# A convolution-then-feed-forward kernel: GpSimd's adds go one to a step, a step behind their products, and VectorE's transposes of x go behind the sum of low parts

## The chip, the cores and the metric

The kernel runs on one core of one Trainium2 chip. The metric is the device time of one execution in microseconds (us), as the median of several runs.

## The reference

The computation is a causal convolution along the sequence with seven softmaxed taps per head, followed by a feed-forward layer with a clipped quadratic between its two matrix products. Cut to what matters (the padding of the sequence's start is in x_pad):

```python
# x [8, 4096, 192], weight [8, 7], w_in [192, 2048], w_out [2048, 192]; 8 heads of 24 channels
w = softmax(weight)                                   # over the 7 taps of each head
x = einsum('hk,bskhg->bshg', w, x_unf)                # x_unf: 7 shifted views of x_pad
x = x.reshape(32768, 192)
h = x @ w_in
g = where(h >= 1, h, where(h <= -1, 0, (h + 1)**2 / 4))
out = g @ w_out
```

## The kernel before, in words

**Steps.** The 32768 tokens are cut into 64 groups of 512 tokens (NSB), and the 2048 hidden columns into 8 pairs of 128 (NPAIR). One step q does one pair of one group, so there are 512 steps. The main loop (L967) counts 16 steps, two groups, as one block c; i is the step within the block. Everything is written out in program order; each engine does its own instructions in that order, and semaphores connect the engines.

**TensorE.** In step q it does `mm1(q)` (L448, matmuls at L475), which makes h of pair q, and then `mm2(q-3)` (L511, matmuls at L528), which adds the product of an older g with w_out into four PSUM banks. Both have 36 matmuls of 64 rows by 512 columns, 18 each, and these run in pairs on the two halves of the rows. Numbers are split into a high and a low part (float32r) to keep precision, so `mm1` reads from the convolved x: for the natural layout "n" hi, hi, lo; for the swapped layout "s" hi, hi, lo; then the rest "r". The swapped tiles are copies of hi and lo with the partition halves exchanged, made by two DMAs on SyncE's queue (`swapped`, L252, issues at L255 and L256). h has two buffers, so `mm1(q+2)` waits until the last reader of h(q) is done.

**What the other engines do in step q.** ScalarE: `act_both(q)` (ReLU at L562, square at L563), at i = 2 and i = 10 four copies out of PSUM (`evac_banks`, L609), the products of the convolution (`product`, L237), then `act_hi(q-1)` (L573: gh). VectorE: `act_low(q-2)` (L579: gl), its share of the convolution, `act_sum(q-2)` (L585: the sum of low parts, tile m), transposes of finished output (L631) at i = 0, 7, 8, 15, then `act_most(q)` (L890), the last reader of h(q).

**The convolution** of the next tokens is spread over the steps by tables (PLAN_B, PLAN_A, PLAN_R, L830 to L833), which name what unit b, a or r of a block does at which i: "T" is the transpose of loaded x (L163, VectorE), a number is a tap, "split" makes the high and low part. Unit a holds the first group of a block, b the second (128 channels each), r the other 64 channels of both. Unit a's taps run on VectorE (L230, L232). For b and r ScalarE makes the product of a tap (L237; tap 0 at L244) and GpSimd adds it to y. `conv_slot` (L842) does what the tables say for a step; from the third block of tokens on, the add isn't written at once but put on the list `held`, and `add_held` (L126) writes it behind `act_sum`, with a dependency on it, so that GpSimd starts the add (L129) only when the sum is done.

**Splits.** `splits` (L263) for units a and b: ScalarE copies y to hi (L268), SyncE swaps hi, GpSimd computes lo = y - hi (L272), SyncE swaps lo. `split_rest` (L278) for unit r: ScalarE's copy rh (L282), VectorE's rl = y - rh (L283), and the swaps. The b split stands at i = 5, the first reader of its tiles is `mm1` at i = 8. The a split stands at i = 12 and the r split at i = 13; their first reader is `mm1` at i = 0 of the next block. GpSimd also issues the accumulating DMAs of `evac_add` (L619) at i = 3, 4, 11 and 12.

Of the kernel before, what the change touches and what calls it, by code (L numbers as in the profile page):

```python
# [8 lines left out]
F32 = mybir.dt.float32  # L9
# [22 lines left out]
def lightconv_then_ffn(ctx: ExitStack, tc: tile.TileContext, x, weight, w_in, w_out, out):  # L32
# [24 lines left out]
    nc = tc.nc  # L57
# [53 lines left out]
    def load_unit(c, u, engs=None):  # L111
        ta, tb = 2 * c * TB, (2 * c + 1) * TB
        if u == "rb":
            return load_raw([tb, tb, tb + TB // 2, tb + TB // 2], [P, P + SQ, P, P + SQ], engs,
                            TB // 2)
        if u == "r":
            return load_raw([ta, ta, tb, tb], [P, P + SQ, P, P + SQ], engs)
        return load_raw([ta if u == "a" else tb] * 4, [0, SQ, 2 * SQ, 3 * SQ], engs)
# [2 lines left out]

    pending = []

    held = []

    def add_held(behind):  # L126

        for out, a, b in held:
            add = nc.gpsimd.tensor_add(out, a, b)  # L129
            if behind is not None:  # L130
                tc.add_manual_dep(add.ins, behind.ins.name, mybir.DependencyInfo(
                    mybir.DependencyClass.Sync, mybir.DependencyReason.DATA), reason="port")
        held.clear()

    def let_go():

# [10 lines left out]
    class Conv:  # L147
# [92 lines left out]
        def taps(self, *ks):  # L240
            y = self.y
            for k in ks:
                if k == 0:
                    nc.scalar.mul(y, self.xT[:, SH:SH + TB], wk[:, self.wsel, 0:1])  # L244
                elif self.c == 1 and self.u != "b":
                    pending.append((y, y, self.product(k)))
                elif self.c > 1:
                    held.append((y, y, self.product(k)))
                else:
                    nc.gpsimd.tensor_add(y, y, self.product(k))  # L250

# [4 lines left out]
            nc.sync.dma_start(out=w[BOT].bitcast(F32), in_=t[TOP].bitcast(F32))  # L256
            return w

        def split(self, eng=None):
            for _ in self.splits(eng or nc.gpsimd):  # L260
                pass

        def splits(self, eng):  # L263

            o = xop[2 * self.c + (self.u == "b")]
            hi = xo.tile([P, TB], F32R, name="hi0")
            lo = xo.tile([P, TB], F32R, name="lo0")
            nc.scalar.copy(hi, self.y)  # L268
            for key, t in (("hi", hi), ("lo", lo)):
                if key == "lo":  # L270
                    yield
                    eng.tensor_sub(lo, self.y, hi.bitcast(F32))  # L272
                w = self.swapped(t, key + "1", 3)
                o["n", key] = (t[TOP], t[BOT])
                o["s", key] = (w[TOP], w[BOT])
            yield

        def split_rest(self):  # L278

# [157 lines left out]
    NQ = NSB * NPAIR  # L437
# [63 lines left out]
    turns = tc.alloc_semaphore("turns")  # L501
# [79 lines left out]
    def act_sum(q):  # L581
        gt = stage.tile([P, CC], F32R, name="m")[:, 0:TB]
        gts[q] = gt
        gl = gls[q].bitcast(F32)
        return nc.vector.tensor_add(gt, gl[:, 0, :], gl[:, 1, :])  # L585
# [214 lines left out]
    def whole(j, *cols):  # L800
        for _ in chunks[j].bits(*cols):
# [19 lines left out]
    conv_b, conv_rb = Conv(0, "b", raw_b), Conv(0, "rb", raw_rb)  # L821
# [5 lines left out]

    PLAN_B = {12: ("T",), 14: (0, 1), 15: (2, 3), 1: (4,), 2: (5,), 3: (6,), 5: "split"}  # L830
    PLAN_A = {1: ("T",), 2: (0,), 4: (1,), 6: (2,), 7: (3,), 9: (4,), 10: (5,), 11: (6,),
              12: "split"}
    PLAN_R = {2: ("T",), 4: (0,), 6: (1,), 7: (2,), 8: (3, 4), 9: (5,), 11: (6,), 13: "split"}  # L833
    SECOND_B = {0: (0, 1), 1: (2,), 2: (3,), 3: (4,), 4: (5, 6), 5: "split"}


# [2 lines left out]
    FIRST_A = {7: ("T", 0, 1, 2), 8: (3, 4), 9: (5, 6), 11: "split"}  # L839
    FIRST_R = {8: ("T",), 9: (0,), 10: (1, 2), 11: (3, 4), 12: (5, 6), 13: "split"}  # L840

    def conv_slot(i, b, a, r):  # L842
        early = b is not None and b.c == 0
        plans = ((None if early else b, SECOND_B if b and b.c == 1 else PLAN_B),
                 (a, FIRST_A if early else PLAN_A),
                 (r, FIRST_R if early else PLAN_R))
        for u, plan in plans:
            what = plan.get(i, ()) if u else ()
            if what == "split":
                if u is r:  # L850
                    u.split_rest()
                else:
                    u.split()
                continue
            if "T" in what:
                u.transpose()
            ks = [k for k in what if k != "T"]
            if ks:
                (u.taps_dve if u is a and not early else u.taps)(*ks)
# [8 lines left out]
    def parts_hi(q):  # L868
        for n, rest in PARTS.get(q, ()):
            chunks[n].hi(rest)  # L870
# [95 lines left out]
    conv_n, ahead = {}, {}  # L966
    for q in range(NQ + LATE):  # L967
        s, j = divmod(q, NPAIR)
        c, i = divmod(q, 2 * NPAIR)
        if q < NQ and i == 0 and c > 0:  # L970
            conv_b = conv_n["b"]
        if q < NQ and i == (0 if c > 0 else 4):
            conv_n, ahead = ahead, {}
            if c > 0 and c + 1 < NB:
                for u in "arb":
                    if u not in conv_n:
                        conv_n[u] = Conv(c + 1, u, load_unit(c + 1, u))
        if c == 0 and i in (4, 5, 10):
            u = {4: "a", 5: "r", 10: "b"}[i]
            conv_n[u] = Conv(1, u, load_unit(1, u))  # L980
        if i == (14 if c == 0 else 8) and c + 2 < NB:
            ahead = {u: Conv(c + 2, u, load_unit(c + 2, u)) for u in "ar"}

        done = q - (DELAY if q < NF32 + DELAY else LATE)
        if done < 0 or q == NF32 + DELAY:
            done = None
        if q == NPAIR:
            mm2_first(done)
        if q < NQ:
            mm1(q)  # L990
        if done is not None and q != NPAIR:
            (pair_last if done == NQ - 1 else mm2 if done >= NF32 else mm2_first)(done)

        if q < 2:
            (step_0, step_1)[q]()
        elif q < NPAIR:
            first_step(q)
        elif q < NF32:
            if q == NPAIR + 1:
                evac(0)  # L1000
            if q == 2 * NPAIR - 2:
                pending.extend(late)
            let_go()
            act_clip(q)
            act_square(q)
            parts_hi(q + 1)
            parts_lo(q, (True,))
            let_go()
            act_max(q)
            parts_lo(q, (False,))  # L1010
            conv_slot(i, conv_b, conv_n.get("a"), conv_n.get("r"))
            if j >= NPAIR - 2:
                store(0, "mr"[j - NPAIR + 2])
        else:
            if q == NQ - 1:
                act_hi(q - 1)
            if q < NQ:
                act_both(q)
            if done is not None and done % NPAIR == NPAIR - 1 and done < NQ - 1:
                (evac if done < NF32 else evac_banks)(done // NPAIR)  # L1020
            if done == NQ - 2:
                evac_last(done // NPAIR)
            if q == NF32:
                parts_lo(q)
            n = q - 1 if q < NF32 + 3 else q - 2
            low = n in ghs and n not in gls
            ahead_of = q in (NF32 + 2, NF32 + 3)
            if low:
                act_low(n)
            if ahead_of:  # L1030
                act_most(q)
            if q < NQ:
                conv_slot(i, conv_b if i < 8 else conv_n.get("b"), conv_n.get("a"),
                          conv_n.get("r"))
            add_held(act_sum(n) if low else None)
            if q == NQ - 1:
                act_low(q - 1)
                act_most(q)
                act_sum(q - 1)
            if q < NQ:  # L1040
                if s > 2 and j in (3, 4):
                    evac_add(s - 1, j - 3)
                if s <= 2 or s == NSB - 1:
                    m = 6 if s > 2 else 2
                    if m <= j < m + 2:
                        store(s - 1, "mr"[j - m])
                elif j == NPAIR - 1:
                    store(s - 1, "m")
                if j == 0 and s > 3:
                    store(s - 2, "r")  # L1050
            if q - 1 in gs and q - 1 not in ghs and q < NQ:
                act_hi(q - 1)
            if q < NQ - 1 and not ahead_of:
                act_most(q)
            if q < NF32 + 2:
                act_hi(q)
        if i == 2 * NPAIR - 1 and c == 0:
            conv_n["b"].transpose()
        if q == NQ - 4:
            plain = ob.tile([P, TB // SQ, SQ], F32, name="osb").rearrange("p j b -> p (j b)")[:, 0:P]  # L1060
            diagonal(plain, 0)
# [26 lines left out]
```

## Time and profile before

| what | value |
|---|---|
| median of 3 runs | 2046.57 us (2046.46 to 2049.79) |
| the profiled execution | 2046.76 us, span 2045.0 us |
| PE (TensorE matmul) busy | 2037.9 us, 100% |
| PEld (TensorE weight load) busy | 1756.9 us, 86% |
| DVE (VectorE) busy | 1966.2 us, 96% |
| ACT (ScalarE) busy | 1960.4 us, 96% |
| POOL (GpSimd) busy | 792.8 us, 39% |
| granted TensorE clock | 1.000 |

The span is from the first to the last instruction; the execution's own time lies 1.8 us above it. Busy time is that in which the engine has an instruction in work; records of neighbouring instructions can overlap by some tens of nanoseconds, and matmuls overlap by design.

### The profile page before, as it was taken

The page shows a single profiled execution, that of the slowest core. Times are in us where ns is not written, and L with a number is a line of the kernel's source. Part 1 is how long each engine was busy: PE and PEld are TensorE (multiplying, and loading weights), DVE is VectorE, ACT ScalarE, POOL GpSimd, SP SyncE. Part 2 cuts the span into 40 slices and gives each one's busy share as a digit, 9 for nine tenths or more (in the row PEclk, how much of TensorE's full clock was granted, in tenths as well). Part 3 has the DMA queues.
Part 4 walks back from the last instruction along what each step waited for, and adds up shares of the span by engine and source line. Part 5 has one row for each costly group of instructions (what it writes and reads, how often), then busy time and mean ns, then how long its engine had stood idle before and what let it go on. Part 6 is the DMA issues. An engine that isn't in the chain of part 4 may idle for free.

```text
span 2045.0 us, 46902 instructions
## 1 busy us (share of the span) xinstructions
PE 2037.9 (100%) x18644; PEld 1756.9 (86%) x18644; DVE 1966.2 (96%) x2109; ACT 1960.4 (96%) x2381; POOL 792.8 (39%) x749
## 2 busy tenths in 40 slices
PE   9999999999999999999999999999999999999999
PEld 6998888888888888888888888888888888888888
DVE  8899999999999999999999999999999999999998
ACT  8799999999999999999999999999999999999997
POOL 1544343343433443334434344343343333443431
PEclk9999999999999999999999999999999999999999
DMA  7333333443434434334333344343343433433323
GB/s 178 80 62 70 69 71 71 85 76 56 81 68 79 80 65 77 71 67 87 70 66 73 72 82 76 57 83 69 74 81 65 76 71 66 86 72 65 72 55 55
DMA packets 470685, 152.27 MB, mean 74 GB/s; under 512 B 418944, under 2 KB 426624, under 8 KB 470464
## 3 DMA queue, kind: packets, MB, share of 16 engines
q1 hardware_dynamic: 446880, 109.17, 25.4%
q0 software_dynamic: 23424, 39.99, 13.4%
q8 instruction: 146, 2.39, 0.5%
q14 instruction: 75, 0.61, 0.1%
q10 hardware_dynamic: 160, 0.10, 0.0%
HBM read 32.84 MB, written 25.17 MB: 28 GB/s over the span
## 4 chain that ended last, share of the span: by engine, by line
PE 68%; DVE 15%; ACT 13%; issue 4%; DVEq 0%; ACTq 0%; POOL 0%; POOLq 0%
PE h L475 35%; PE accr L528 20%; PE accm L528 10%; DVE gl L579 7%; DVE g L890 4%; ACT gh L573 3%; ACT g L562 3%; ACT g L563 3%; DVE m L585 3%; ACT p L237 3%; DVE osb L631 1%; PE accm L495 1%; PE accr L495 1%; ACT t L609 0%; ACT y L244 0%
## 5 line engine op out<-in xcount | busy, mean ns | idle before, releaser
L579 DVE TENSOR_TENSOR gl<-g,gh 128x1024 fp32r<-128x1024 f32 x495 | 728.1, 1471 | 23.4 <-ACT gh L573 17.1
L890 DVE SCALAR_TENSOR_TENSOR g<-g,h 128x1024 f32<-128x1024 f32 x504 | 607.5, 1206 | 4.8 <-ACT g L563 2.8
L475 PE MATMUL h<-hi,w 64*128 64x512 f32 x4032 | 609.4, 380 | 1.5
L528 PE MATMUL accr<-gh,wg 64*128 64x512 f32 x3960 | 590.1, 376 | 0.0
L562 ACT ACTIVATE g<-h 128x1024 f32<-128x1024 f32 (+1 forms) x497 | 507.2, 1020 | 41.6 <-PE h L475 39.9
L563 ACT ACTIVATE g<-g 128x1024 f32<-128x1024 f32 (+1 forms) x497 | 526.6, 1060 | 15.8
L573 ACT CAST gh<-g 128x1024 fp32r<-128x1024 f32 x495 | 514.4, 1039 | 0.5 <-DVE g L890 0.4
L129 POOL TENSOR_TENSOR y<-y,p 128x512 f32<-128x512 f32 x180 | 231.0, 1283 | 573.3 <-ACT p L237 300.5
L475 PEld LDWEIGHTS h<-hi,w 64*128 64x128 f32 x4032 | 376.0, 186 | 76.4 <-DVE g L890 28.2
L528 PEld LDWEIGHTS accr<-gh,wg 64*128 64x128 f32 x3960 | 373.9, 185 | 53.2
L129 POOL TENSOR_TENSOR r<-r,p 128x512 f32<-128x512 f32 x180 | 232.5, 1291 | 476.6 <-DVE m L585 420.0
L475 PE MATMUL h<-lo,w 64*128 64x512 f32 x2016 | 383.8, 376 | 0.0
L528 PE MATMUL accr<-gl,words 64*128 64x512 f32 x1980 | 376.3, 376 | 0.0
L585 DVE TENSOR_TENSOR m<-gl 128x512 fp32r<-128x512 f32 x495 | 348.0, 703 | 20.6 <-PE h L475 0.5
L528 PE MATMUL accm<-gh,wg 64*128 64x512 f32 x1980 | 295.1, 376 | 0.0
L475 PE MATMUL h<-rh,w 64*128 64x512 f32 x992 | 293.6, 376 | 0.0
L475 PE MATMUL h<-rhi,w 64*128 64x512 f32 x992 | 293.6, 376 | 0.0
L619 POOL DMA_DIRECT2D t<-t x244 | 206.0, 983 | 97.6 <-DMA t<-t 75.6
L475 PEld LDWEIGHTS h<-lo,w 64*128 64x128 f32 x2016 | 192.2, 186 | 25.9
L528 PEld LDWEIGHTS accr<-gl,words 64*128 64x128 f32 x1980 | 188.3, 186 | 26.0
L528 PEld LDWEIGHTS accm<-gh,wg 64*128 64x128 f32 x1980 | 188.0, 186 | 26.0
L475 PEld LDWEIGHTS h<-rhi,w 64*128 64x128 f32 x992 | 184.5, 186 | 12.9
(161 smaller groups left out, 2313.3 us busy)
## 6 DMA issues: line engine op xcount, KB each, us to landing
t<-t POOLq DMA_DIRECT2D x183, 128.0 KB, 4.1
out_dram<-osb SPq DMA_DIRECT2D x366, 64.0 KB, 1.9
raw<-in_x_dram SPq DMA_DIRECT2D x334, 68.0 KB, 2.6
hi<-hi SPq DMA_DIRECT2D x128, 128.0 KB, 3.4
lo<-lo SPq DMA_DIRECT2D x126, 128.0 KB, 3.1
t<-t POOLq DMA_DIRECT2D x61, 256.0 KB, 3.3
rhi<-rh SPq DMA_DIRECT2D x62, 128.0 KB, 4.1
rlo<-rl SPq DMA_DIRECT2D x62, 128.0 KB, 3.5
```

Of the source, the lines that this page charges most:

```text
L129: add = nc.gpsimd.tensor_add(out, a, b)
L237: nc.scalar.mul(p, self.xT[:, SH + k:SH + k + TB], wk[:, self.wsel, k:k + 1])
L475: nc.tensor.matmul(h[e], w[HALVES[e], c0:c0 + P], seen(x[e][e]), start=(n == 0), stop=(n == len(mms) - 1))
L495: nc.tensor.matmul(accs[s][a, i][:, c0:c0 + D], block, w[half, e, :], start=(j == 0 and e == 0 and b % 2 == 0), stop=(j == NPAIR - 1 and e ...
L528: mm = nc.tensor.matmul(accs[s][bank], w[half], in_turn(g[half]), start=(j == 0 and bank not in seen), stop=(j == NPAIR - 1 and k % 3 == 2 ...
L562: nc.scalar.activation(g[:, e, :], hs[q][:, e, :], AF.Relu, bias=0.5, scale=0.5)
L563: nc.scalar.activation(g[:, e, :], g[:, e, :], AF.Square)
L573: nc.scalar.copy(gh[:, e, :], gs[q][:, e, :])
L579: nc.vector.tensor_sub(gl[:, e, :], g[:, e, :], gh[:, e, :])
L585: return nc.vector.tensor_add(gt, gl[:, 0, :], gl[:, 1, :])
L619: nc.gpsimd.dma_start(out=to, in_=src, accum_op=ALU.add)
L890: nc.vector.scalar_tensor_tensor(out=g, in0=g, scalar=1.0, in1=h, op0=ALU.min, op1=ALU.max)
```

## The change

Three things change, all from the third block of tokens on.

1. Every GpSimd add or subtraction of the convolution is put on the list `fresh`, and moves to `held` when a step ends. So it is written one step after its product, behind that step's `act_sum`, and waits for this sum. This now holds for the lo subtraction of the a and b splits too (with the swap of lo behind it): b's goes from i = 5 to i = 6, a's from i = 12 to i = 13.
2. The tables give at most one product to a step, but for i = 14, where tap 0 is a plain product into y: b's tap 3 goes from i = 15 to i = 0; r's tap 4 from i = 8 to i = 9, and its tap 5 from i = 9 to i = 10.
3. `conv_slot` is called twice in a step: before `add_held` for all but the entries with "T", and behind it for those. So the transpose of loaded x stands behind the sum of low parts.

```diff
--- before.py
+++ after.py
@@ -121,16 +121,17 @@
 
     pending = []
 
-    held = []
+    held, fresh = [], []
 
     def add_held(behind):
 
-        for out, a, b in held:
-            add = nc.gpsimd.tensor_add(out, a, b)
+        for work in held:
+            done = work()
             if behind is not None:
-                tc.add_manual_dep(add.ins, behind.ins.name, mybir.DependencyInfo(
+                tc.add_manual_dep(done.ins, behind.ins.name, mybir.DependencyInfo(
                     mybir.DependencyClass.Sync, mybir.DependencyReason.DATA), reason="port")
-        held.clear()
+        held[:] = fresh
+        fresh.clear()
 
     def let_go():
 
@@ -245,7 +246,7 @@
                 elif self.c == 1 and self.u != "b":
                     pending.append((y, y, self.product(k)))
                 elif self.c > 1:
-                    held.append((y, y, self.product(k)))
+                    fresh.append(lambda p=self.product(k): nc.gpsimd.tensor_add(y, y, p))
                 else:
                     nc.gpsimd.tensor_add(y, y, self.product(k))
 
@@ -256,9 +257,15 @@
             nc.sync.dma_start(out=w[BOT].bitcast(F32), in_=t[TOP].bitcast(F32))
             return w
 
-        def split(self, eng=None):
-            for _ in self.splits(eng or nc.gpsimd):
-                pass
+        def split(self):
+
+            if self.c < 2:
+                for _ in self.splits(nc.gpsimd):
+                    pass
+                return
+            parts = self.splits(nc.gpsimd)
+            next(parts)
+            fresh.append(lambda: next(parts))
 
         def splits(self, eng):
 
@@ -266,14 +273,15 @@
             hi = xo.tile([P, TB], F32R, name="hi0")
             lo = xo.tile([P, TB], F32R, name="lo0")
             nc.scalar.copy(hi, self.y)
+            sub = None
             for key, t in (("hi", hi), ("lo", lo)):
                 if key == "lo":
                     yield
-                    eng.tensor_sub(lo, self.y, hi.bitcast(F32))
+                    sub = eng.tensor_sub(lo, self.y, hi.bitcast(F32))
                 w = self.swapped(t, key + "1", 3)
                 o["n", key] = (t[TOP], t[BOT])
                 o["s", key] = (w[TOP], w[BOT])
-            yield
+            yield sub
 
         def split_rest(self):
 
@@ -827,10 +835,11 @@
 
 
 
-    PLAN_B = {12: ("T",), 14: (0, 1), 15: (2, 3), 1: (4,), 2: (5,), 3: (6,), 5: "split"}
+    PLAN_B = {12: ("T",), 14: (0, 1), 15: (2,), 0: (3,), 1: (4,), 2: (5,), 3: (6,), 5: "split"}
     PLAN_A = {1: ("T",), 2: (0,), 4: (1,), 6: (2,), 7: (3,), 9: (4,), 10: (5,), 11: (6,),
               12: "split"}
-    PLAN_R = {2: ("T",), 4: (0,), 6: (1,), 7: (2,), 8: (3, 4), 9: (5,), 11: (6,), 13: "split"}
+    PLAN_R = {2: ("T",), 4: (0,), 6: (1,), 7: (2,), 8: (3,), 9: (4,), 10: (5,), 11: (6,),
+              13: "split"}
     SECOND_B = {0: (0, 1), 1: (2,), 2: (3,), 3: (4,), 4: (5, 6), 5: "split"}
 
 
@@ -839,13 +848,15 @@
     FIRST_A = {7: ("T", 0, 1, 2), 8: (3, 4), 9: (5, 6), 11: "split"}
     FIRST_R = {8: ("T",), 9: (0,), 10: (1, 2), 11: (3, 4), 12: (5, 6), 13: "split"}
 
-    def conv_slot(i, b, a, r):
+    def conv_slot(i, b, a, r, turns=None):
         early = b is not None and b.c == 0
         plans = ((None if early else b, SECOND_B if b and b.c == 1 else PLAN_B),
                  (a, FIRST_A if early else PLAN_A),
                  (r, FIRST_R if early else PLAN_R))
         for u, plan in plans:
             what = plan.get(i, ()) if u else ()
+            if turns is not None and turns != ("T" in what):
+                continue
             if what == "split":
                 if u is r:
                     u.split_rest()
@@ -1030,9 +1041,11 @@
             if ahead_of:
                 act_most(q)
             if q < NQ:
-                conv_slot(i, conv_b if i < 8 else conv_n.get("b"), conv_n.get("a"),
-                          conv_n.get("r"))
+                units = conv_b if i < 8 else conv_n.get("b"), conv_n.get("a"), conv_n.get("r")
+                conv_slot(i, *units, turns=False)
             add_held(act_sum(n) if low else None)
+            if q < NQ:
+                conv_slot(i, *units, turns=True)
             if q == NQ - 1:
                 act_low(q - 1)
                 act_most(q)
```

How this moves instructions is seen at three places, one on each of three engines. In the rows lines of the changed kernel have other numbers: L249 is the add of before's L129, L280 the lo subtraction of L272, L627 the accumulating DMA of L619, L617 the copy out of PSUM of L609, L238 the product of L237, L581 gh of L573, L570 and L571 ReLU and square of L562 and L563, L275 and L290 the copies hi and rh of L268 and L282, L256 and L257 the swaps of L255 and L256.

GpSimd's queue before, from b's split at i = 5 to a's split at i = 12 of one block (r and y are the tiles that taps are added to, p a product, t the finished sums; DVE, Activation, Pool in the brackets are the engines waited for):

```order
L272 TENSOR_TENSOR lo_8939<-y,hi_8938 128x512 [waits DMAHW4_49,DMAHW5_49,PE_49,Activation_49]
L129 TENSOR_TENSOR r<-r,p 128x512 [waits DVE_49,Activation_49]
L129 TENSOR_TENSOR r<-r,p 128x512 [waits DVE_49,Activation_49,Pool_49] x2
L129 TENSOR_TENSOR r<-r,p 128x512 [waits Activation_49,Pool_49]
L129 TENSOR_TENSOR r<-r,p 128x512 [waits DVE_49,Activation_49,Pool_49] x2
L619 DMA t<-t 128x512 [waits DMASW7_49,DMASW6_49]
L619 DMA t<-t 64x512 [waits DMASW1_49]
L272 TENSOR_TENSOR lo_9352<-y,hi_9351 128x512 [waits DMAHW6_49,DMAHW7_49,PE_49,Activation_49]
```

The same stretch of GpSimd's queue in the changed kernel:

```order
L280 TENSOR_TENSOR lo_8939<-y,hi_8938 128x512 [waits DMAHW0_49,DMAHW1_49,DVE_49,Activation_49]
L249 TENSOR_TENSOR r<-r,p 128x512 [waits DVE_49,Activation_49]
L249 TENSOR_TENSOR r<-r,p 128x512 [waits DVE_49,Activation_49,Pool_49] x4
L627 DMA t<-t 128x512 [waits DMASW7_49,DMASW6_49]
L627 DMA t<-t 64x512 [waits DMASW1_49]
L249 TENSOR_TENSOR r<-r,p 128x512 [waits DVE_49,Activation_49,Pool_49]
L627 DMA t<-t 64x512 [waits DMASW0_49]
L627 DMA t<-t 64x512
L280 TENSOR_TENSOR lo_9348<-y,hi_9347 128x512 [waits DMAHW6_49,DMAHW7_49,DVE_49,Activation_49]
```

The lo subtraction waits for VectorE where it did not, and the add that had no wait for VectorE (the second of a step) has one. The last add of r goes behind the first two accumulating DMAs, and a's lo subtraction behind all four.

ScalarE's queue before, at i = 10 of one block, where the four copies out of PSUM stand, and up to r's split at i = 13:

```order
L563 ACTIVATE g<-g 128x1024
L609 COPY t<-accr_6934 128x512
L609 COPY t<-accr_6935 128x512
L609 COPY t<-accm_6932 128x512
L609 COPY t<-accm_6933 128x512
L573 CAST gh<-g 128x1024
L562 ACTIVATE g<-h 128x1024
L563 ACTIVATE g<-g 128x1024
L237 ACTIVATE p<-r,wk 128x512
L573 CAST gh<-g 128x1024
```

ScalarE's queue in the changed kernel, the same place:

```order
L571 ACTIVATE g<-g 128x1024
L617 COPY t<-accr_6933 128x512
L617 COPY t<-accr_6934 128x512
L617 COPY t<-accm_6931 128x512
L617 COPY t<-accm_6932 128x512
L238 ACTIVATE p<-r,wk 128x512
L581 CAST gh<-g 128x1024
L570 ACTIVATE g<-h 128x1024
L571 ACTIVATE g<-g 128x1024
L238 ACTIVATE p<-r,wk 128x512
L581 CAST gh<-g 128x1024
```

One product more stands between the copies and gh; it came from i = 9.

SyncE's queue before, the swaps at i = 12 and 13 of one block:

```order
L255 DMA hi_7484<-hi_7481 64x512 [waits DMAHW2_49,PE_49,Activation_49]
L256 DMA hi_7484<-hi_7481 64x512 [waits DMAHW3_49]
L255 DMA lo_7488<-lo_7482 64x512 [waits DMAHW4_49,PE_49,Pool_49]
L256 DMA lo_7488<-lo_7482 64x512 [waits DMAHW5_49]
L255 DMA rhi<-rh 64x512 [waits DMAHW6_49,PE_49,Activation_49]
L256 DMA rhi<-rh 64x512 [waits DMAHW7_49]
L255 DMA rlo<-rl 64x512 [waits DMAHW0_49,DVE_49,PE_49]
L256 DMA rlo<-rl 64x512 [waits DMAHW1_49]
```

And in the changed kernel:

```order
L256 DMA hi_7480<-hi_7477 64x512 [waits DMAHW2_49,PE_49,Activation_49]
L257 DMA hi_7480<-hi_7477 64x512 [waits DMAHW3_49]
L256 DMA rhi<-rh 64x512 [waits DMAHW4_49,PE_49,Activation_49]
L257 DMA rhi<-rh 64x512 [waits DMAHW5_49]
L256 DMA rlo<-rl 64x512 [waits DMAHW6_49,DVE_49,PE_49]
L257 DMA rlo<-rl 64x512 [waits DMAHW7_49]
L256 DMA lo_7551<-lo_7478 64x512 [waits DMAHW0_49,Pool_49]
L257 DMA lo_7551<-lo_7478 64x512 [waits DMAHW1_49]
```

The swap of a's lo goes behind the swaps of rh and rl.

## Rows read from the trace of the kernel before

**Rows 1.** Windows (us; PE, PEld, DVE, ACT, POOL busy, count): steady stretch; i = 3 to 7, block 13.

```profile
150.00:1900.00 1750.00, 1747.42 (x16030) 1507.45 (x16028) 1701.09 (x1754) 1702.31 (x2032) 693.67 (x635) 1.00 0.39 73
849.89:869.31 19.42, 19.42 (x182) 17.02 (x180) 18.79 (x20) 19.26 (x25) 8.52 (x8) 1.00 0.36 62
```

**Rows 2.** Waits, whole run: engine line <- releaser: us in total, times, longest.

```profile
PEld h L475 <- DVE g L890: 28.2, 83, 0.5
DVE rl L283 <- ACT rh L282: 15.0, 21, 1.0
```

**Rows 3.** Groups by line, whole run: busy us, mean ns of one.

```profile
L579 DVE TENSOR_TENSOR gl<-g,gh 128x1024 fp32r<-128x1024 f32 x495 | 728.1, 1471 | 23.4 <-ACT gh L573 17.1
```

**Rows 4.** Timeline, turn from block 12 to 13: start us, us, engine [idle before <-releaser].

```profile
839.32 2.65 POOL L129 TENSOR_TENSOR y<-y,p 128x512 f32<-128x512 f32 x2 [2.16 <-ACT p L237]
840.77 2.28 DVE L579 TENSOR_TENSOR gl<-g,gh 128x1024 fp32r<-128x1024 f32 x1
845.76 1.22 DVE L579 TENSOR_TENSOR gl<-g,gh 128x1024 fp32r<-128x1024 f32 x1
845.89 0.30 PEld L475 LDWEIGHTS h<-hi,w 64*128 64x128 f32 x4 [0.45 <-DVE g L890]
```

**Rows 5.** Timeline, b's split in block 13 to the first mm1 that reads it.

```profile
863.29 1.04 ACT L573 CAST gh<-g 128x1024 fp32r<-128x1024 f32 x1
863.47 1.28 POOL L272 TENSOR_TENSOR lo<-y,hi 128x512 fp32r<-128x512 f32 x1 [0.23 <-ACT hi L268]
864.36 1.47 DVE L579 TENSOR_TENSOR gl<-g,gh 128x1024 fp32r<-128x1024 f32 x1
864.83 1.82 SPq L255 DMA_DIRECT2D lo<-lo  x1
865.75 0.74 DVE L232 SCALAR_TENSOR_TENSOR y<-xT,wk,y 128x512 f32<-128x512 f32 x1
866.41 0.68 DVE L585 TENSOR_TENSOR m<-gl 128x512 fp32r<-128x512 f32 x1
867.24 1.28 POOL L129 TENSOR_TENSOR r<-r,p 128x512 f32<-128x512 f32 x1 [2.49 <-DVE m L585]
869.31 0.59 PE L475 MATMUL h<-hi,w 64*128 64x512 f32 x4
870.39 0.38 PE L475 MATMUL h<-lo,w 64*128 64x512 f32 x2
```

**Rows 6.** Tile lo, 150 to 1900 us: first swap's issue (ns, min/median/max), both swaps' landing.

```profile
L255 SPq DMA_DIRECT2D lo<-lo x56: 461/502/1817, 173.8 to 1899.2; - x56
DMA to landing us min/median/max: 2.2/3.1/4.2
```

**Rows 7.** Timeline of ACT, ReLUs of i = 2 to 6 and i = 10 in block 13.

```profile
848.15 1.02 ACT L562 ACTIVATE g<-h 128x1024 f32<-128x1024 f32 x1 [0.54 <-PE h L475]
853.63 1.05 ACT L562 ACTIVATE g<-h 128x1024 f32<-128x1024 f32 x1
857.22 1.01 ACT L562 ACTIVATE g<-h 128x1024 f32<-128x1024 f32 x1
860.78 1.01 ACT L562 ACTIVATE g<-h 128x1024 f32<-128x1024 f32 x1
864.24 1.01 ACT L562 ACTIVATE g<-h 128x1024 f32<-128x1024 f32 x1
879.23 1.02 ACT L562 ACTIVATE g<-h 128x1024 f32<-128x1024 f32 x1
```

**Rows 8.** Timeline, r's split (i = 13) in block 11, and mm1 of i = 15.

```profile
765.06 1.01 ACT L562 ACTIVATE g<-h 128x1024 f32<-128x1024 f32 x1
767.70 0.69 DVE L283 TENSOR_TENSOR rl<-r,rh 128x512 fp32r<-128x512 f32 x1 [0.73 <-ACT rh L282]
768.91 1.21 DVE L890 SCALAR_TENSOR_TENSOR g<-g,h 128x1024 f32<-128x1024 f32 x1
770.42 0.59 PE L475 MATMUL h<-hi,w 64*128 64x512 f32 x4
```

## The prediction

> **What bounds the kernel now.** Begin with the table: all of TensorE, VectorE and ScalarE are busy for 96% or more at a full clock, so look next at how evenly TensorE's steps follow each other. The windows give that. In the steady stretch 16030 matmuls take 1750 us; at 36 to a step that is 3.930 us a step, 62.88 us a block of 16. The five steps of block 13 in the second row take 19.42 us, 3.885 us each, with TensorE busy throughout: this is a step in which nothing makes it wait [rows 1]. So stalls are worth 16 x 0.045 = 0.72 us a block, some 22 us in all (31 blocks have the full program). This is all that any relief of VectorE, ScalarE or GpSimd can give back; the rest is matmul work that the change leaves alone.
>
> The waits tell where the stalls come from. TensorE's weight loads wait 83 times for `act_most` on VectorE, 28.2 us [rows 2] (more than the stalls, since a weight load normally sits a little ahead of its matmul). Why VectorE is late is seen at the turn of a block: two adds follow each other on GpSimd, 2.65 us, and gl, which takes 1.22 us when GpSimd is quiet, takes 2.28 us beside them; two steps later TensorE waits for `act_most` [rows 4]. Over the run gl takes 1.47 us in the mean [rows 3].
>
> **The change, part by part.** Four things are priced: what VectorE gets back, what the later lo of unit b costs, what the product moved to i = 10 costs, and the later lo of unit a.
>
> *VectorE.* A GpSimd operation costs it what is left of that operation when gl wants to start: in block 13 gl starts at 864.36, the lo subtraction runs to 864.75 (863.47 + 1.28), and gl takes 1.47 us [rows 5] instead of 1.22, 0.25 more; behind two adds it takes 2.28, 1.06 more [rows 4]. An add that the sum releases starts 0.15 us behind its end (866.41 + 0.68 = 867.09, to 867.24) and also takes 1.28 us [rows 5], so it outlasts `act_most` a little, and I price it at the same 0.25. After the change no step has two adds: two steps a block (i = 8 and 15) gain 0.8 each. A transpose between sum and `act_most` (0.73 us by its shape's neighbour, the tap at 865.75 [rows 5], which has as many elements) covers what the add has left: three steps (i = 1, 2, 12) gain 0.25. That is 2.4 us of VectorE a block. It lies off TensorE's path except in the stalls, so its worth is between nothing and 0.72 us; since the stall that the rows show comes from such a pair, I take all of it: **-0.72 us a block**. The transposes themselves are first read a step or two later, under work of those steps; without that cover each would cost its 0.7 us.
>
> *The later lo of unit b.* Before, the lo subtraction starts at 863.47, when the cast hi is done, and its first swap is issued at 864.83. Its first swapped reader is `mm1` of i = 8, which starts at 869.31 and comes to the swapped lo with its sixth pair of matmuls, at 870.39 [rows 5]: the lo had time to spare. After the change it waits for the sum of the next step, at 866.41 in this block. That sum can move forward only a little: gl starts at 864.36, as soon as ScalarE's gh ends (863.29 + 1.04), and this stays. Without GpSimd beside it gl takes 1.22 us, so tap and sum come 0.25 us earlier and the sum ends at 866.84. GpSimd then starts at 866.99, ends at 868.27; SyncE issues 0.08 us later, 868.35, as at 864.83 [rows 5]. An issue takes 0.50 us [rows 6], so the second swap goes out at about 868.90. Landing takes 2.2 to 4.2 us, 3.1 in the middle [rows 6]. At 2.2 us it lands at 871.10 and TensorE stalls 0.7 us; at 3.1 us, 1.6 us. I take 2.4 us, since the swaps of hi and the accumulating DMAs, beside which the old ones ran, are through by then: 871.30, a stall of 0.9 us, and an estimated 0.1 us to be at pace again (the weight loads that end such a wait take 0.30 us for four [rows 4], and part of that lies open): **+1.0 us a block**. No other engine's slack can hide this: TensorE works its queue in order, and the rest of `mm1` and `mm2` stands behind that pair. On GpSimd only r's first add, a step later, stands behind the wait, and on SyncE the stores of i = 7: nobody waits for those. The Trainium skill, DMA: Bandwidth & Descriptors, section "Anatomy of one DMA", gives 2.0 us fixed plus bytes over 436 GB/s, fitted for DMAs that GpSimd issues; for these 128 KB that is an estimate of 2.3 us. By it the stall would be 0.8 + 0.1 us, 3 us less over the run; the trace's least, 2.2, agrees, its median doesn't, and I go by the rows.
>
> *The product at i = 10.* ScalarE comes to i = 2 idle, waiting for h (its ReLU at 848.15), and its next ReLU comes 5.48 us later: the four copies and a product. Steps with a product then take 3.59 (853.63 to 857.22), the step with the cast hi 3.46 (860.78 to 864.24) [rows 7]. At i = 10 it starts as promptly: at i = 2 its ReLU is 1.74 us ahead of the next `mm1` (848.15 to 849.89 [rows 1, 7]), and 869.31 + 3 x 3.885 - 1.74 is 879.23, where the ReLU stands [rows 7]. But before the change it has the copies without a product; with the change it has both, so it should run as at i = 2: ReLUs of 11, 12 and 13 at 5.48, 9.07 and 12.53 us after that of 10. Unit r's split follows the ReLU of 13: rl starts 2.64 us behind it (765.06 to 767.70), having waited for rh, and `act_most` ends 5.06 us behind it (768.91 + 1.21) [rows 8], so at 17.59. TensorE would start `mm1` of i = 15 unhindered at 21.16 - 3.885 = 17.28: from the ReLU of i = 2 to `mm1` of i = 8 it is 869.31 - 848.15 = 21.16 us [rows 5, 7], and 10 to 15 is one step less. A stall of 0.31 us, and with the release and the same refilling some 0.15 more: **+0.46 us a block**. In block 11 before, the same chain ended 0.30 us ahead of `mm1` (770.12 to 770.42) [rows 8].
>
> *The later lo of unit a* goes behind the swaps of rh and rl on SyncE's queue. In the times of the last paragraph, counted from the ReLU of i = 10, rl starts at 15.17 and `act_most` 1.21 later (767.70 to 768.91 [rows 8]), at 16.38, about when the sum ends; 0.15 + 1.28 for the subtraction, 0.08 + 0.50 to the second issue and 3.1 to land give 21.5. `mm1` of the next block's i = 0 would start unhindered at 21.16, six steps behind that ReLU, and comes to swapped lo 1.08 later (869.31 to 870.39 [rows 5]), at 22.24. So I take nothing; at 4.2 us, the longest landing [rows 6], it would be 0.4 us a block.
>
> *The sum.* -0.72 + 1.0 + 0.46 = +0.74 us a block; 30 blocks have the new order: +22 us on a span of 2045.0. With the 1.8 us around it, which also brings the profiled execution to the median shown, **2069 us**.
>
> **The rivals.**
> - *Only the lo swap counts.* If ScalarE recovers more before i = 13, the second stall is gone: -0.72 + 1.0 = +0.28, 8 us more, 2055. For it: TensorE's first stall in the block gives every engine 1.0 us; against it: ScalarE comes to i = 10 idle either way.
> - *Slow landings.* At the median of 3.1 us instead of 2.4 the swap costs 1.7 us: +1.44 a block, 43 us, 2090. For it: the median is measured; against it: those DMAs shared the queues.
> - *The swap is hidden: faster.* If the second swap lands within 1.5 us of its issue (870.39 - 868.90), or TensorE comes to `mm1` of i = 8 0.9 us later for a reason that I don't see, only the second stall stays: -0.26 a block, 2039; without it too, -0.72, 2025. Against it: no landing of lo took under 2.2 us [rows 6].
> - *Nothing changes.* The least landing (0.7 us) and no second stall: +0.0, 2047. For it: each size is within its rows; against it: both must hold.
>
> **How the numbers follow.** Both waits as sized: 0.55. Only the lo swap: 0.16. Slow landings: 0.09. Faster: 0.10 (0.06 at 2039, 0.04 at 2025). Nothing: 0.10. A measurement of this kernel can tell 0.2%, about 4 us, from no change. So faster 0.10, same 0.10, slower 0.80. The range goes from the case of nothing, 2046, to 2086, where landings take about 2.9 us and the second stall stands; the faster cases and the slowest landings are left out.
>
> **What would show it.** The lo subtraction starts right behind the sum of i = 6, some 2.3 us before `mm1` of i = 8. TensorE waits for the DMA lo there in every block, 25 to 35 us in all, the longest in its list of waits. rl waits for rh in every block, about 1 us each time, against 15.0 us in 21 waits before [rows 2]. TensorE waits for `act_most` at i = 15, and no longer at i = 2. gl's mean falls from 1.47 us to about 1.3. The prediction is wrong if TensorE has no wait for lo, because the sum comes earlier than I let it or because swaps alone on the queues land in well under 2.2 us; and its size is wrong with the landing.

## The result and the profile after

| | before | after |
|---|---|---|
| median of 5 runs | 2046.77 us (2046.46 to 2049.79) | 2064.92 us (2064.30 to 2065.30) |
| span of the profiled execution | 2045.0 us | 2063.1 us |
| PE, DVE, ACT, POOL busy | 100%, 96%, 96%, 39% | 100%, 91%, 95%, 38% |

The changed kernel is slower: ratio 1.0086, 95% interval 1.0073 to 1.010, 18 us. 2069 us was forecast.

The window of the steady stretch in the changed kernel (columns as in [rows 1]):

```profile
150.00:1900.00 1750.00, 1745.73 (x15869) 1573.55 (x15867) 1597.96 (x1738) 1686.96 (x2011) 679.92 (x627) 1.00 0.40 72
```

15869 matmuls at 36 to a step make 3.970 us a step, 63.52 us a block, against 62.88 before and 62.16 without stalls. So stalls went from 0.72 to 1.36 us a block, 0.64 more. The starts of `mm1` in the trace say where (from each to the next, less 3.885 us, as a mean over blocks 2 to 30): the changed kernel loses 0.78 us a block at i = 8, 0.47 at i = 14 and 0.10 at i = 15, and next to nothing elsewhere. VectorE's share fell and TensorE's stayed at 100%: a pipelined engine that waits half a microsecond here and there still counts as busy, and the count of matmuls in a stretch tells more than the share.

The waits of the changed kernel name what stands where. Beside them gl's group (columns as in [rows 2] and [rows 3]):

```profile
DVE rl L291 <- ACT rh L290: 25.7, 31, 1.0
PEld h L483 <- DMA lo<-lo: 24.5, 59, 0.5
PEld h L483 <- DVE g L901: 12.5, 31, 0.5
PEld accm L536 <- DVE m L593: 10.2, 30, 0.3
```

```profile
L587 DVE TENSOR_TENSOR gl<-g,gh 128x1024 fp32r<-128x1024 f32 x495 | 634.9, 1283 | 118.5 <-ACT gh L581 113.9
```

TensorE's 83 waits for `act_most` are down to 31, one a block. The wait for the DMA lo is new (59 times, two a block), and the sum m is now late once in every block (before: `PEld accm L528 <- DVE m L585: 8.5, 22, 0.6`). gl is down from 1.47 to 1.28 us, so VectorE got back what it was to get; it now stands idle 113.9 us for ScalarE's gh.

The first stall, as the timeline of block 13 shows it, i = 6 to the end of i = 8:

```profile
871.11 1.04 ACT L581 CAST gh<-g 128x1024 fp32r<-128x1024 f32 x1
872.19 1.23 DVE L587 TENSOR_TENSOR gl<-g,gh 128x1024 fp32r<-128x1024 f32 x1
873.33 0.74 DVE L233 SCALAR_TENSOR_TENSOR y<-xT,wk,y 128x512 f32<-128x512 f32 x1
873.99 0.68 DVE L593 TENSOR_TENSOR m<-gl 128x512 fp32r<-128x512 f32 x1
874.81 1.28 POOL L280 TENSOR_TENSOR lo<-y,hi 128x512 fp32r<-128x512 f32 x1 [3.97 <-ACT p L238]
876.12 0.46 SPq L256 DMA_DIRECT2D lo<-lo  x1
876.62 0.60 SPq L257 DMA_DIRECT2D lo<-lo  x1
877.13 0.60 PE L483 MATMUL h<-hi,w 64*128 64x512 f32 x4
878.36 0.18 PEld L483 LDWEIGHTS h<-lo,w 64*128 64x128 f32 x1 [0.39 <-DMA lo<-lo]
878.98 0.18 PEld L483 LDWEIGHTS h<-lo,w 64*128 64x128 f32 x1 [0.44 <-DMA lo<-lo]
881.78 0.70 PE L483 MATMUL h<-hi,w 64*128 64x512 f32 x4
```

Read it from the top: gh ends, gl starts at once, tap, sum. The subtraction starts 0.14 us behind the sum's end (874.67); the trace puts this down to a product of ScalarE that ended between, but that isn't an operand of the subtraction, which waits for the cast hi, done in the step before, and for the sum. Two swaps go out. The sixth pair of matmuls is due at 877.13 + 1.08 = 878.21, and its weight loads wait for the first swap and then for the second, until 878.98. `mm1` of the next step comes 4.65 us later instead of 3.885. The swaps now go out when those of hi are through, and they land sooner than before, with a median of 2.3 us instead of 3.1 (tile lo, 150 to 1900 us):

```profile
DMA to landing us min/median/max: 2.2/2.3/4.3
```

The second stall, block 13, from the ReLU of i = 10 to `mm1` of the next i = 0:

```profile
887.92 1.02 ACT L570 ACTIVATE g<-h 128x1024 f32<-128x1024 f32 x1 [0.23 <-PE h L483]
893.39 1.05 ACT L570 ACTIVATE g<-h 128x1024 f32<-128x1024 f32 x1
896.98 1.01 ACT L570 ACTIVATE g<-h 128x1024 f32<-128x1024 f32 x1
900.45 1.01 ACT L570 ACTIVATE g<-h 128x1024 f32<-128x1024 f32 x1
901.21 0.70 PE L483 MATMUL h<-hi,w 64*128 64x512 f32 x4
903.09 0.69 DVE L291 TENSOR_TENSOR rl<-r,rh 128x512 fp32r<-128x512 f32 x1 [0.82 <-ACT rh L290]
904.30 1.21 DVE L901 SCALAR_TENSOR_TENSOR g<-g,h 128x1024 f32<-128x1024 f32 x1
904.44 0.19 PEld L536 LDWEIGHTS accm<-m,words 64*128 64x128 f32 x2 [0.34 <-DVE m L593]
905.57 0.30 PEld L483 LDWEIGHTS h<-hi,w 64*128 64x128 f32 x4 [0.40 <-DVE g L901]
909.56 0.59 PE L483 MATMUL h<-hi,w 64*128 64x512 f32 x4
```

ScalarE's ReLUs come 5.47, 3.59 and 3.47 us apart, rl waits for rh, and behind rl both the sum and `act_most` are late for TensorE. `mm1` of i = 14, 15 and 0 start at 901.21, 905.57 and 909.56: 4.36 and 3.99 us instead of 3.885, 0.58 together.

### The profile page after: what moved, and what is told of

Its sections match the earlier page's. It is cut to its first block, busy times and chain, and to the rows that moved or that the text cites. A ratio compares the mean times of both kernels' runs of the same rounds, so it can differ in the third digit from the quotient of the medians.

```text
span 2063.1 us, 46868 instructions
## 1 busy us (share of the span) xinstructions
PE 2054.3 (100%) x18644; PEld 1841.6 (89%) x18644; DVE 1871.6 (91%) x2109; ACT 1962.2 (95%) x2381; POOL 785.3 (38%) x749
## 4 chain that ended last, share of the span: by engine, by line
PE 67%; ACT 14%; DVE 9%; issue 4%; DMA 3%; POOL 2%; SPq 1%; ACTq 0%; DVEq 0%; POOLq 0%
PE h L483 34%; PE accr L536 20%; PE accm L536 10%; DVE gl L587 5%; ACT gh L581 4%; DMA lo<-lo 3%; ACT p L238 3%; ACT g L570 3%; ACT t L617 2%; POOL lo L280 2%; DVE g L901 2%; DVE y L233 1%; DVE m L593 1%; PE accm L503 1%; PE accr L503 1%
## 5 line engine op out<-in xcount | busy, mean ns | idle before, releaser
L587 DVE TENSOR_TENSOR gl<-g,gh 128x1024 fp32r<-128x1024 f32 x495 | 634.9, 1283 | 118.5 <-ACT gh L581 113.9
L536 PE MATMUL accr<-gh,wg 64*128 64x512 f32 x3960 | 635.9, 377 | 0.0
L570 ACT ACTIVATE g<-h 128x1024 f32<-128x1024 f32 (+1 forms) x497 | 507.1, 1020 | 57.2 <-PE h L483 57.1
L571 ACT ACTIVATE g<-g 128x1024 f32<-128x1024 f32 (+1 forms) x497 | 525.8, 1058 | 15.8
L581 ACT CAST gh<-g 128x1024 fp32r<-128x1024 f32 x495 | 512.5, 1035 | 0.5 <-DVE g L901 0.4
L483 PEld LDWEIGHTS h<-hi,w 64*128 64x128 f32 x4032 | 418.6, 186 | 47.5 <-DVE g L901 12.5
L536 PEld LDWEIGHTS accr<-gh,wg 64*128 64x128 f32 x3960 | 406.5, 185 | 38.1
L483 PE MATMUL h<-lo,w 64*128 64x512 f32 x2016 | 435.1, 379 | 4.5 <-DMA lo<-lo 2.2
L249 POOL TENSOR_TENSOR y<-y,p 128x512 f32<-128x512 f32 x180 | 231.3, 1285 | 522.4 <-DVE m L593 269.0
L536 PE MATMUL accr<-gl,words 64*128 64x512 f32 x1980 | 419.0, 376 | 0.0
L249 POOL TENSOR_TENSOR r<-r,p 128x512 f32<-128x512 f32 x180 | 231.7, 1287 | 459.6 <-DVE m L593 269.5
L483 PEld LDWEIGHTS h<-lo,w 64*128 64x128 f32 x2016 | 231.7, 186 | 40.1 <-DMA lo<-lo 24.5
L536 PEld LDWEIGHTS accr<-gl,words 64*128 64x128 f32 x1980 | 230.2, 186 | 16.2
L536 PEld LDWEIGHTS accm<-gh,wg 64*128 64x128 f32 x1980 | 215.2, 186 | 16.3
L627 POOL DMA_DIRECT2D t<-t x244 | 206.6, 983 | 31.3 <-ACT t L617 16.3
L536 PE MATMUL accm<-m,words 64*128 64x512 f32 x990 | 213.9, 382 | 0.0
```

The costliest lines, as they stand in the source:

```text
L249: fresh.append(lambda p=self.product(k): nc.gpsimd.tensor_add(y, y, p))
L483: nc.tensor.matmul(h[e], w[HALVES[e], c0:c0 + P], seen(x[e][e]), start=(n == 0), stop=(n == len(mms) - 1))
L536: mm = nc.tensor.matmul(accs[s][bank], w[half], in_turn(g[half]), start=(j == 0 and bank not in seen), stop=(j == NPAIR - 1 and k % 3 == 2 ...
L570: nc.scalar.activation(g[:, e, :], hs[q][:, e, :], AF.Relu, bias=0.5, scale=0.5)
L571: nc.scalar.activation(g[:, e, :], g[:, e, :], AF.Square)
L581: nc.scalar.copy(gh[:, e, :], gs[q][:, e, :])
```

## The experiments

Theory: the time lost is the sum of two waits that the change makes, one for b's swapped lo (4.65 - 3.885 = 0.77 us a block) and one for r's rl (0.58 us), each with its own cause; the old stalls are gone. The expectations put the two at 0.755 and 0.57 us. The rival in each case is that a wait only takes the place of another engine's lateness, or that its cause is another part of the change. Ratios are to the kernel before, run beside each.

### b's lo at once

```diff
         def split(self):
-            if self.c < 2:
+            if self.c < 2 or self.u == "b":
                 for _ in self.splits(nc.gpsimd):
                     pass
                 return
```

> The changed kernel, with unit b's lo subtraction and its swap back at i = 5, in one go with the cast, as before the change; all else as changed. Theory (two new waits, each at its own price): the wait for the DMA lo at i = 8, 0.755 us a block in the changed kernel's trace, goes, and the 0.57 us at i = 14 and 15 stay: 2064.9 - 30 x 0.755 = 2042 us (2038 to 2046), no wait of TensorE for lo. Rival (the wait for lo only takes the place of VectorE's lateness, which comes back at i = 9 to 13 when it is gone): 2050 to 2062 us, with TensorE's waits for act_most up by 10 us or more.

Measured: 2039.85 us (2039.69 to 2040.03), ratio 0.9966 (0.9954 to 0.9978). The window of the steady stretch and TensorE's waits:

```profile
150.00:1900.00 1750.00, 1749.99 (x16086) 1526.94 (x16086) 1622.56 (x1760) 1710.42 (x2040) 689.41 (x636) 1.00 0.41 73
```

```profile
PEld h L483 <- DVE g L901: 12.5, 31, 0.5
PEld accm L536 <- DVE m L593: 10.6, 30, 0.4
```

The wait for lo is gone, and what stays are the 31 and 30 waits of the second stall. 16086 matmuls are 62.67 us a block, 0.51 above the stall-free 62.16. With this one line undone the rest of the change is a gain: 25 us less than the changed kernel.

### b's lo a step later, but without the dependency on the sum

```diff
-            if behind is not None:
+            if behind is not None and work not in free:
                 tc.add_manual_dep(done.ins, behind.ins.name, ...)
...
             fresh.append(lambda: next(parts))
+            if self.u == "b":
+                free.append(fresh[-1])
```

`free` is a new list, empty at first; what stands in it does not wait for the sum.

> The changed kernel; unit b's lo subtraction still written a step later, but without the dependency on the sum, so that it starts when ScalarE's cast hi is done. Theory (the wait for the sum is what makes the swap late): as with b's lo at once, 2040 us (2038 to 2043), the wait of TensorE for lo gone. Rival (the later place in the queues of GpSimd and SyncE makes it late, not the wait): 2060 to 2066 us.

Measured: 2039.71 us (2039.11 to 2041.02), ratio 0.9965 (0.9952 to 0.9978), no wait of TensorE for lo. So it is not the place in the queues but the wait for the sum that makes the swap late.

### r's table of before

```diff
-    PLAN_R = {2: ("T",), 4: (0,), 6: (1,), 7: (2,), 8: (3,), 9: (4,), 10: (5,), 11: (6,),
-              13: "split"}
+    PLAN_R = {2: ("T",), 4: (0,), 6: (1,), 7: (2,), 8: (3, 4), 9: (5,), 11: (6,), 13: "split"}
```

> The changed kernel with unit r's table of before: taps 3 and 4 both at i = 8, tap 5 at i = 9, none at i = 10; adds a step behind, so two of them at i = 9. Theory: ScalarE's product behind the four copies at i = 10 is the cause of the waits at i = 14 and 15, so they go, 0.57 us a block: 2064.9 - 17 = 2048 us (2045 to 2053; the two adds at i = 9 may give some of it back), and rl waits for rh much less than 25.7 us. Rival (VectorE itself is late there, by the adds and the transpose moved behind the sum): 2062 to 2067 us, rl's wait as long as now.

Measured: 2050.47 us (2049.82 to 2051.13), ratio 1.0016 (1.0007 to 1.0026). TensorE's and VectorE's waits:

```profile
DVE rl L291 <- ACT rh L290: 29.4, 31, 1.0
PEld h L483 <- DMA lo<-lo: 24.8, 58, 0.7
PEld h L483 <- DVE g L900: 0.7, 2, 0.5
```

The second stall is gone with the product at i = 10, and only the one for lo is left, now up to 0.7 us in one wait: by the starts of `mm1`, i = 8 loses 0.90 us a block instead of 0.78, and no other step loses time. In one thing the expectation missed: rl's wait for rh is not shorter but longer, 29.4 us. It is no measure of the stall: VectorE comes to rl earlier and waits longer, while rh itself is done 1.25 us behind the start of `mm1` of i = 14 in the median, not 1.85 as in the changed kernel, early enough for TensorE.

### r's table of the change on the kernel before

The same edit the other way round, on the kernel before, whose adds stand in their own step.

> The kernel before with unit r's table of the change alone (one tap at i = 8, 9, 10, 11 each; adds in their own step, lo at once, transposes in front). Theory (the product behind the four copies at i = 10 is enough to make rh, rl and act_most of i = 13 late): waits of 0.57 us a block at i = 14 and 15 as in the changed kernel, against some 0.4 us that one add at i = 8 and the later cast of hi at i = 12 give back: 2051 us (2046 to 2058). Rival (the product only hurts together with adds that come a step later): 2034 to 2041 us.

Measured: 2048.66 us (2048.16 to 2049.35), ratio 1.0008 (0.9998 to 1.0018). Its waits:

```profile
PEld h L475 <- DVE g L891: 38.4, 106, 0.8
DVE rl L283 <- ACT rh L282: 22.7, 31, 1.0
PEld accm L528 <- DVE m L585: 4.0, 26, 0.2
```

Inside the theory's bounds and outside the rival's: the product makes the lateness without any add behind its step. TensorE waits 106 times for `act_most` instead of 83. By the starts of `mm1` it loses 0.49 us a block at i = 12 to 15, not at i = 14 and 15 alone. Before, it lost 0.23 there, through sums held up at i = 12 (see the transposes alone, below), and none is held up here. What the second add at i = 8 cost before, 0.21 us at i = 9 to 11, is saved but for 0.02, and the product takes it back.

### Both tables of before

Both tables set back in the changed kernel, which leaves the adds a step behind and the transposes behind the sum.

> The changed kernel with both tables of before (unit b's taps 2 and 3 at i = 15, unit r's 3 and 4 at i = 8): adds a step behind their products, two of them at i = 0 and i = 9, lo behind the sum, transposes behind the sum. Theory: the wait for lo stays as with unit r's table alone, and VectorE has a microsecond to spare at i = 0 to 2 for the second add: 2050 us (2048 to 2054). Rival (two adds in a step cost a stall wherever they stand): 2057 to 2062 us.

Measured: 2050.19 us (2050.03 to 2050.81), ratio 1.0018 (1.0009 to 1.0028), as with r's table alone. Two adds in one step, a step later, cost TensorE nothing here; whether they would without its wait for lo was not tried.

### The transposes alone

The third part of the change by itself on the kernel before: `conv_slot` in two halves around `add_held`.

> The kernel before with the third part of the change alone: transposes of loaded x behind the sum of low parts. Theory: VectorE gains about 0.25 us at i = 1 and 2, but TensorE's wait at the turn of a block comes from the two adds at i = 15, earlier; at i = 12 the transpose stands behind a sum that the lo subtraction still holds up: 2044 to 2048 us, no difference that can be told. Rival (the transposes in front of the sum are what makes act_most late): 2035 to 2041 us.

Measured: 2039.44 us (2039.14 to 2041.05), ratio 0.9962 (0.9950 to 0.9974). The theory was wrong and the rival right in size. The theory had named the place that matters, i = 12, but took the sum to be held up there with or without the move. In the kernel before, at i = 12 of block 12, with TensorE's `mm1` of i = 13 and its waits behind the sum:

```profile
825.59 0.59 PE L475 MATMUL h<-hi,w 64*128 64x512 f32 x4
826.32 0.73 DVE L163 STREAM_TRANSPOSE xT<-raw 128x544 f32<-128x544 f32 x1
826.92 1.37 POOL L272 TENSOR_TENSOR lo<-y,hi 128x512 fp32r<-128x512 f32 x1
826.98 1.87 DVE L585 TENSOR_TENSOR m<-gl 128x512 fp32r<-128x512 f32 x1
828.90 0.19 PEld L528 LDWEIGHTS accm<-m,words 64*128 64x128 f32 x2 [0.53 <-DVE m L585]
830.04 0.30 PEld L475 LDWEIGHTS h<-hi,w 64*128 64x128 f32 x4 [0.40 <-DVE g L890]
```

With the transposes alone moved, the same place in the same block, where TensorE has no such wait:

```profile
825.87 0.69 DVE L585 TENSOR_TENSOR m<-gl 128x512 fp32r<-128x512 f32 x1
826.28 1.43 POOL L272 TENSOR_TENSOR lo<-y,hi 128x512 fp32r<-128x512 f32 x1
826.48 0.74 DVE L163 STREAM_TRANSPOSE xT<-raw 128x544 f32<-128x544 f32 x1
```

In front of the sum the transpose took just so long that the sum came 0.06 us behind a's lo subtraction and waited it out, 1.87 us instead of 0.69. Ten sums of the 495 took over 1.8 us in the kernel before, none with the transposes moved: there the sum is 0.40 to 0.69 us ahead of the subtraction in every block, and the transpose, at 0.74 us, is not held up beside it. That makes 62.66 us a block (16088 matmuls in the same 1750 us) instead of 62.88, 7 of the 22 us of old stalls.

The starts of `mm1` show that these ten sums are the cause. In each of the ten blocks TensorE loses some 0.57 us at i = 13 (825.59 to 830.04 above: 4.45 us instead of 3.885) and 0.10 at i = 14, 6.7 us together. In the other nineteen of blocks 2 to 30 it loses nothing there, and with the transposes moved in no block. At i = 1 and 2, where the other transposes moved, it loses 0.32 us a block in both kernels, so the 0.25 us that the prediction gave to each of those brought TensorE nothing.

### b's lo at once, and r's taps at i = 5 to 9

```diff
-            if self.c < 2:
+            if self.c < 2 or self.u == "b":
...
-    PLAN_R = {2: ("T",), 4: (0,), 6: (1,), 7: (2,), 8: (3,), 9: (4,), 10: (5,), 11: (6,),
-              13: "split"}
+    PLAN_R = {2: ("T",), 4: (0,), 5: (1,), 6: (2,), 7: (3,), 8: (4,), 9: (5,), 11: (6,),
+              13: "split"}
```

> The changed kernel with b's lo at i = 5 at once, and unit r's taps 1 to 5 at i = 5 to 9, so that no step has two adds and i = 10 has no product. Theory: both waits go and nothing comes in their place, since no step has two adds: 62.2 us a block, 2064.9 - 30 x 1.32 = 2025 us (2022 to 2031), faster than the kernel before by 1%. Rival (ScalarE and VectorE, at 95% and 91%, are the bound as soon as these waits go): 2035 to 2045 us with TensorE's waits for act_most above 15 us.

Measured: 2025.27 us (2024.59 to 2025.53), ratio 0.9892 (0.9875 to 0.9909): 1.1% faster than the kernel before, 1.9% faster than the changed one. The window of the steady stretch:

```profile
150.00:1900.00 1750.00, 1750.00 (x16218) 1530.14 (x16216) 1634.26 (x1776) 1721.21 (x2054) 693.36 (x639) 1.00 0.41 74
```

16218 matmuls are 3.885 us a step, as in the five steps without a wait [rows 1]. Nothing came in place of the two waits, though ScalarE is busy for 98% of this stretch.

### The same, with the transposes in front of the sum

```diff
-                conv_slot(i, *units, turns=False)
+                conv_slot(i, *units)
             add_held(act_sum(n) if low else None)
-            if q < NQ:
-                conv_slot(i, *units, turns=True)
```

> The version with b's lo at once and unit r's taps at i = 5 to 9 (2025.3 us), its transposes of loaded x in front of the sum again. Theory: without two adds in a step VectorE has room for the 0.25 us that each of three adds then costs it: 2025 to 2027 us. Rival (the transposes' place is worth as much here as it was on the kernel before, 7.6 us): 2031 to 2035 us.

Measured: 2026.09 us (2025.90 to 2026.34), ratio 0.9899 (0.9884 to 0.9913). With a's lo behind the sum no sum is held up at i = 12 any more (none of the 495 took over 0.8 us), and the transposes' place is worth under 1 us.

## Why the prediction was right, point by point

- *What bounds it* was right: all that the change could give back was 0.72 us a block, and the version without both waits gives back just that, 2046.8 to 2025.3 us.
- *VectorE's gain* had the right worth and only part of the right cause. All of the 0.72 us went. But the prediction laid it to steps with two adds. By the starts of `mm1` the kernel before loses 0.32 us a block at i = 1 and 2, behind the two adds of i = 15; 0.21 at i = 9 to 11, behind those of i = 8; and 0.23 at i = 13 and 14, through the sums that a's lo subtraction held up at i = 12, which the prediction did not look at. The last goes with the transposes alone, and the second with r's table alone. The first goes with the whole change, and no run shows by itself that the two adds made it; with both tables of before, two adds standing a step later, it is gone too. So that the total came out right was partly luck: the bound was right, and what lay under it was not all of one kind.
- *b's lo*: the chain held link by link, and the wait for the sum is shown as its cause by taking away that wait alone. The size was too large, 1.0 against 0.77 us. The second swap was issued 1.59 us ahead of its need (876.62 to 878.21), not 1.49; TensorE went on 2.36 us behind that (878.98), where 2.4 was taken; and the 0.1 us for getting back to pace was not seen. The Trainium skill, DMA: Bandwidth & Descriptors, section "Anatomy of one DMA", gave an estimate of 2.3 us for the landing, by a fit for DMAs that GpSimd issues, and the trace after agrees with its median of 2.3; for the swaps of the kernel before, with a median of 3.1, it is too short.
- *The product at i = 10*: ReLUs at 5.48, 9.07 and 12.53 us were foreseen and came at 5.47, 9.06 and 12.53; rl and `act_most` followed at 2.64 and 5.06 us as foreseen. The size was too small, 0.46 against 0.58 us, since TensorE was due earlier than reckoned: `mm1` of i = 15 unhindered at 901.21 + 3.885 = 905.10, 17.18 us behind the ReLU of i = 10 and not 17.28. `act_most` ended at 17.59 as forecast; `mm1` started 0.06 us behind it, and the step after took another 0.10, together about what the prediction had put at 0.15. The sum m is late for `mm2` too, but the wait for `act_most` ends last. Moving the product away takes the stall away, and on the kernel before it makes one.
- *a's later lo* was hidden, as foreseen: the version without both waits still has it and runs at 62.2 us a block, with no wait of TensorE for lo. With b's lo alone at once TensorE waited for a lo one single time, 0.4 us.
- *The sum*: -0.72 + 0.77 + 0.58 = 0.63 us a block, 30 blocks, 19 us; 18 measured, 22 forecast. The rest of the new waits' list came as named, but TensorE's wait for lo is 24.5 us where 25 to 35 was said.

## What to carry to other kernels

When work is moved behind a release, follow its results to their first reader, DMA and all, and not only the engine that it is to relieve: the subtraction started 5.84 us ahead of the `mm1` that reads it before (863.47 to 869.31) and 2.32 us after (874.81 to 877.13), 3.5 us later where 2.75 would have been free. Before moving a piece of work one step on, look at what that step has already: one product more cost 0.58 us a block in the step with four copies, and nothing at i = 5 to 9. And split such a change: of its parts, one alone gave 0.4%, and with two lines undone or moved the whole gave 1.1%.

## What the runs showed of the hardware that was not expected

Who waits for whom between VectorE and GpSimd was decided by a few hundredths of a microsecond. In the ten blocks in which the sum (two inputs in SBUF) started 0.05 to 0.09 us behind a's lo subtraction, it took 1.86 to 1.90 us instead of 0.69: in block 12 the 1.31 us that were left of the subtraction, and 0.56 more. Where it started at most 0.03 us behind it, or ahead, it took 0.64 to 0.65 us, and the subtraction could take longer instead, as in block 13 of the kernel before, 1.55 us instead of 1.28:

```profile
890.15 0.64 DVE L585 TENSOR_TENSOR m<-gl 128x512 fp32r<-128x512 f32 x1
890.39 1.55 POOL L272 TENSOR_TENSOR lo<-y,hi 128x512 fp32r<-128x512 f32 x1 [0.22 <-ACT hi L268]
```

At i = 13 and 14, TensorE was late only in the blocks of the first kind.
